# Filter maxima after the plain tiles, earlier transforms, a pipelined inverse, merged butterflies and row stores on GpSimd, in a fused FFT filter and feed-forward kernel

## The chip, the cores and the metric

The kernel runs on one core of a Trainium2 chip. Its engines are TensorE (PE, with its weight loads as PEld), VectorE (DVE), ScalarE (ACT), GpSimd (POOL) and SyncE (SP); SP, ACT and POOL also issue DMAs, each in its own order. The metric is device time in microseconds (us): the median of repeated executions on the same chip. One execution more is profiled; all rows of the profile come from that one.

## The reference

```python
def _A_ref(x, w_r, w_i):
    X = jnp.fft.rfft2(x, axes=(-2, -1))
    X = X * (w_r + 1j * w_i)
    return jnp.fft.irfft2(X, s=(S, D), axes=(-2, -1))

def _B_ref(x, w1, w2):
    h = _silu(jnp.einsum("bsd,df->bsf", x, w1))
    return jnp.einsum("bsf,fd->bsd", h, w2)

xn = _layernorm(x)                 # x: 1 x 2048 x 1024
s = _A_ref(xn, A_w_r, A_w_i)       # filters: 2048 x 513
g = _silu(_B_ref(xn, B_w1, B_w2))  # w1: 1024 x 3584, w2: 3584 x 1024
return x + s * g
```

All is float32. The kernel works on float16 pairs: each operand is split into a high and a low half, and three of the four products are added up in float32.

## The kernel before

**Feed-forward, first layer.** The 2048 tokens are four chunks c of 512, the 3584 hidden columns 28 tiles f of 128. The first 16 tiles are *plain tiles* (`mm1`, L597): for each (c, f) one psum tile pa of 24 matmuls. The other 12 are done by Strassen's scheme (`product`, L635): unit (q, g), with q from 8 to 13 and g the half of the tokens, has seven products M1 to M7 of 12 matmuls each into the psum tiles pa, pe and pc, 84 in all. M2, M3 and M1 use the normalized tokens; M4 to M7 need sums and differences of them, `T[g]`, which `t_gen` makes on DVE (L1414 to L1426) and ACT (L1427) in four rounds for each g. M1's result is copied by ACT from pa to pc (L647), and M6 goes on in pa only after that. Results pass through SiLU (ACT), DVE sums (L687 to L690) and a split (L267 on ACT, L270 on DVE), and are stored to the hd arrays by POOL.

**Second layer.** `mm2` (L737 to L739) takes pb of (m, j), seven output forms m by eight j, each in two halves k of 21 matmuls. `acc` puts the results together with the parts pd that earlier forms left (`load_parts`, L730), and `finish_out` (L811, L812) multiplies by the spatial rows s, adds x and stores the output rows (L814). For the last form m = 6 these stores and the loads of pd, of s (fs) and of x (fx) all stand on SP.

**Spatial part.** The forward transform is `fd_gen` (psum fa, by chunk) and `f_gen` (psum fx, 16 steps u of 36 matmuls, with the filter tiles xn<-in_A_w loaded by L1177 and multiplied on DVE, GpSimd and ACT). Step u is part j = u % 4 of line block q = u // 4. The last of the 513 columns, for the last block, is loaded by itself into xsv (L1179). The inverse is `i_gen(c)`, run for chunks c in the order 1, 3, 0, 2: four iu pieces (24 matmuls, two psum buffers, read by DVE L1475 and L1476), then four id pieces (24), each followed by a butterfly (L1517 to L1533, 14 DVE instructions) and the rows' stores. Its input's edge column is put in by a GpSimd copy from zp (L1456).

**Scales.** The float16 split needs the largest magnitude of each weight and filter. `wmax_gen` loads the filters as 36 pieces of 128x456, mostly two at a time, and reduces them on DVE (L1112). `w2max_gen` loads W2 in 28 tiles of 256 KB, two at a time, makes magnitudes on DVE and ACT and stores sums (L481 to L484). `w2_scales` needs the maxima of W2 before the second layer's weights can be split (`w2_gen`, tiles w2t; its loads are L535 on SP and L540 on POOL).

**What sets the order.** The program is written out by one planner in the order of PE's work. After each psum tile, `work` takes one step of the weight queue `wq`, one of `xq` (maxima) and of `sq`, and then up to three steps of `bg`, the background queue with ln, T, forward and inverse generators in this order; each step yields the DVE time that it is thought to cost, and `bg` goes on only while DVE's modelled clock is at most LEAD = 2.5 us ahead of PE's. Every engine and every DMA queue executes its own instructions strictly in the order written. So a generator that is moved in the plan moves all its instructions on all queues. `t_gen` of g = 1 may start its fourth round only when 8 plain tiles are left (`plain[0]`).

## Time and profile before

| | |
|---|---|
| median of 3 timed runs | 1318.17 us (1311.06 to 1318.68) |
| profiled execution, its own time | 1323.54 us |
| its span | 1321.8 us |
| mean granted clock of TensorE | 0.973 |
| PE busy | 1250.7 us (95%) |
| DVE busy | 996.8 us (75%) |
| ACT busy | 566.7 us (43%) |
| POOL busy | 262.7 us (20%) |
| HBM traffic | 239 GB/s over the span |

The plain tiles end at 380.3 us of the span, the Strassen products at 626.6, and the last matmul at 1304.8. Rows of a timeline read: start us, length us, engine, line, operation, output<-input (partitions x elements, type), count, and in brackets the idle time of the engine before it and what ended this. Rows of waits read: engine, tile and line, what was waited for, us in total, times, longest. A matmul's busy time has a modelled end, so the pitch of rows is a better duration than the busy time.

### The profile page before, as it was taken

The page shows a single profiled execution, that of the slowest core. Times are in us where ns is not written, and L with a number is a line of the kernel's source. Part 1 is how long each engine was busy: PE and PEld are TensorE (multiplying, and loading weights), DVE is VectorE, ACT ScalarE, POOL GpSimd, SP SyncE. Part 2 cuts the span into 40 slices and gives each one's busy share as a digit, 9 for nine tenths or more (in the row PEclk, how much of TensorE's full clock was granted, in tenths as well). Part 3 has the DMA queues.
Part 4 walks back from the last instruction along what each step waited for, and adds up shares of the span by engine and source line. Part 5 has one row for each costly group of instructions (what it writes and reads, how often), then busy time and mean ns, then how long its engine had stood idle before and what let it go on. Part 6 is the DMA issues. An engine that isn't in the chain of part 4 may idle for free.

```text
span 1321.8 us, 18630 instructions
## 1 busy us (share of the span) xinstructions
PE 1250.7 (95%) x6827; PEld 646.1 (49%) x6827; DVE 996.8 (75%) x1708; ACT 566.7 (43%) x844; POOL 262.7 (20%) x406
## 2 busy tenths in 40 slices
PE   8998999999996899999999999999899999999994
PEld 5534445444442344444545455555454455666563
DVE  6677799886997677787487859997798268687685
ACT  4854354353644788976323223332333132322221
POOL 1211253342531223332200000101126001010000
PEclk9998999999997999999999999999899989899997
DMA  7568499678546588866846688989999978685847
GB/s 239 127 171 213 125 293 310 204 177 246 134 101 148 182 256 263 274 200 213 308 143 206 203 275 207 318 233 291 224 320 293 373 251 305 231 305 213 310 139 254
DMA packets 181611, 306.68 MB, mean 232 GB/s; under 512 B 32528, under 2 KB 86288, under 8 KB 180368
## 3 DMA queue, kind: packets, MB, share of 16 engines
q1 hardware_dynamic: 137360, 169.62, 41.5%
q0 software_dynamic: 28368, 87.05, 23.6%
q10 hardware_dynamic: 15792, 48.83, 10.6%
q8 instruction: 53, 0.87, 0.3%
q14 instruction: 38, 0.31, 0.1%
HBM read 204.25 MB, written 111.67 MB: 239 GB/s over the span
## 4 chain that ended last, share of the span: by engine, by line
PE 43%; DMA 15%; DVE 7%; ACT 4%; issue 3%; POOL 1%; SPq 0%; ACTq 0%; DVEq 0%; POOLq 0%
PE pb L737 8%; PE pb L738 8%; PE pb L739 8%; PE pa L635 7%; DMA r<-in_B_w_dram 5%; PE pe L635 3%; PE iu L1466 3%; DMA pl<-pd 3%; PE fx L1193 1%; DMA xn<-vd 1%; PE id L1495 1%; PE pc L635 1%; DMA sd<-xn 1%; DMA out_dram<-pl 1%; DVE r L1419 1%
## 5 line engine op out<-in xcount | busy, mean ns | idle before, releaser
L597 PE MATMUL pa<-xn,w 128*128 128x512 f16 x1536 | 337.7, 382 | 8.8 <-DMA xn<-xs 3.7
L737 PE MATMUL pb<-r,w 128*128 128x512 f16 (+1 forms) x798 | 299.8, 376 | 0.0
L738 PE MATMUL pb<-r,w 128*128 128x512 f16 (+1 forms) x798 | 299.7, 376 | 0.0
L739 PE MATMUL pb<-r,w 128*128 128x512 f16 (+1 forms) x798 | 299.5, 375 | 0.0
L597 PEld LDWEIGHTS <-w 128*128 128x128 f16 x1536 | 150.8, 99 | 192.5 <-issue 11.8
L635 PEld LDWEIGHTS <-w 128*128 128x128 f16 x1008 | 99.7, 99 | 146.6 <-issue 25.7
L739 PEld LDWEIGHTS <-w 128*128 128x128 f16 x798 | 78.1, 98 | 91.3 <-issue 0.3
L635 PE MATMUL pa<-r,w 128*128 128x512 f16 x432 | 104.0, 390 | 18.6 <-ACT r L1427 7.7
L737 PEld LDWEIGHTS <-w 128*128 128x128 f16 x798 | 78.3, 98 | 87.6 <-issue 0.2
L738 PEld LDWEIGHTS <-w 128*128 128x128 f16 x798 | 78.2, 98 | 87.4
L267 ACT ACTIVATE r<-r,sc 128x512 f16<-128x512 f32 x88 | 61.1, 716 | 100.0 <-DMA r<-in_B_w_dram 70.7
L270 DVE SCALAR_TENSOR_TENSOR r<-r,sc 128x512 f16<-128x512 f32 x88 | 64.6, 745 | 29.1 <-ACT r L267 29.1
L681 POOL DMA_DIRECT2D hd_one<-hoone x52 | 49.4, 949 | 139.6 <-DVE hoone L270 80.3
L681 POOL DMA_DIRECT2D hd_sum<-hosum x52 | 42.0, 912 | 169.9 <-DVE hosum L270 104.4
L270 DVE SCALAR_TENSOR_TENSOR hoone<-h,hs,hoone 128x2048 f16<-128x2048 f32 x28 | 65.7, 2346 | 12.7 <-ACT hoone L267 12.5
L607 ACT ACTIVATE h<-pa,ep 128x512 f32<-128x512 f32 x64 | 43.3, 679 | 67.5 <-PE pa L597 65.3
L687 DVE TENSOR_TENSOR hr<-h 128x1024 f32<-128x1024 f32 x28 | 34.2, 1222 | 44.0 <-ACT h L607 25.9
L267 ACT ACTIVATE hoone<-h,hs 128x2048 f16<-128x2048 f32 x28 | 55.9, 1995 | 17.2 <-DMA hd_one<-hoone 15.5
L1466 PE MATMUL iu<-xn 128*128 128x256 f16 x384 | 50.6, 298 | 9.2 <-DVE xn L1476 6.2
L267 ACT ACTIVATE hosum<-hr,hs 128x1536 f16<-128x1536 f32 x28 | 43.9, 1569 | 23.7 <-DVE hr L688 13.4
L540 POOL DMA_DIRECT2D r<-in_B_w_dram x28 | 24.1, 880 | 143.3 <-DMA r<-in_B_w_dram 142.0
L1193 PE MATMUL fx<-xn 128*128 128x256 f16 x192 | 45.4, 281 | 7.2 <-DVE r L1305 5.3
(293 smaller groups left out, 2079.1 us busy)
## 6 DMA issues: line engine op xcount, KB each, us to landing
r<-in_B_w_dram SPq DMA_DIRECT2D x74, 256.0 KB, 6.8
w<-hd_dif ACTq DMA_DIRECT2D x32, 448.0 KB, 5.7
w<-hd_sum ACTq DMA_DIRECT2D x32, 448.0 KB, 6.5
w<-hd_one ACTq DMA_DIRECT2D x32, 448.0 KB, 7.2
hd_sum<-hosum POOLq DMA_DIRECT2D x52, 256.0 KB, 5.2
hd_one<-hoone POOLq DMA_DIRECT2D x52, 256.0 KB, 5.0
hd_dif<-hoone POOLq DMA_DIRECT2D x52, 256.0 KB, 4.8
xn<-in_B_w_dram SPq DMA_DIRECT2D x38, 256.0 KB, 4.1
```

Source lines behind the costliest of these rows:

```text
L267: nc.scalar.activation(hi, raw, AF.Copy, scale=scale)
L270: nc.vector.scalar_tensor_tensor(lo, raw, scale, hi, op0=OP.mult, op1=OP.subtract)
L597: nc.tensor.matmul(ps, w[:, wh, d], xt[:, xh, d], start=(n == 0), stop=(n == 23))
L607: nc.scalar.activation(hq[:, 2 * (c % 2) + f % 2], ps, AF.Silu, scale=ep[:, q:q + 1])
L635: nc.tensor.matmul(ps, lhs(d, wh), rhs(d, xh), start=(name in ("M1", "M5") and d + n == 0), stop=(d + n == 5), skip_group_check=True)
L681: defer(1, lambda k=k, m=m: stores[0].dma_start(hd[m, g][:, :, q].rearrange("f p h s -> f p (h s)"), o[:, k].rearrange("f p h s -> f p (h ...
L687: tt(sums[:, 0:2], hq[:, 0::2], hq[:, 1::2], op=OP.subtract)
L737: nc.tensor.matmul(ps, hh[:, 0], w[:, 0], start=first, stop=False)
L738: nc.tensor.matmul(ps, hh[:, 0], w[:, 1], start=False, stop=False)
L739: nc.tensor.matmul(ps, hh[:, 1], w[:, 0], start=False, stop=last)
L1193: nc.tensor.matmul(o, k[:, c, kh, 1], v[:, c, vh], start=(n == 0), stop=False)
L1466: nc.tensor.matmul(ps[:, q], lhs, rhs, start=(n == 0 and r == 0), stop=(n == 2 and r == 1))
```

## The change

Eight edits, all in one version.

1. `wmax_gen` is put on a queue of its own, `yq`, and is added when T is done (it was added at the seventh plain tile). It takes single pieces of 456 elements in two fixed buffers. `w2max_gen`, which came behind it in `xq`, so starts in the plain stage, and its Strassen part has two pairs of buffers for three, with one more step between.
2. T, which stands behind the forward transforms of the first chunks in `bg`, comes earlier, since these are partly issued ahead: `fa_mat` and `fa_evac` of the first pieces of chunks 1 and 3 are written into the end of the chunk before, and since the reductions of the filter maxima no longer take DVE's modelled time.
3. `f_gen`'s parts of the last block are taken in the order 3, 0, 1, 2 (`part_of`), and the last part is loaded with 129 columns, so that the two separate loads of one column (L1179) are dropped.
4. The inverse becomes one generator over all chunks: the first pieces of the next chunk are issued with the last ones of the one before, and the zp copy with piece 3. While it runs (`fine`), `mm2` is written in groups of 12 and 9 matmuls with one background step between.
5. The butterfly is written in 8 DVE instructions.
6. Output rows of full width are stored by POOL; half rows stay on SP and ACT.
7. `load_parts` for m = 6 is called one j ahead, and stores that are held are written out before it.
8. The loads of a chunk's zt come one step sooner.

```diff
@@ w2max_gen
-            state[1] += 2
+            state[1] += 1
+            load()
+            if aux[1] == 2:
+                yield 0
+            state[1] += 1
@@ load_parts, mm2
     def load_parts(m, j):
+        while m == 6 and held.get("pt"):
+            d = held["pt"][0]
+            slow.remove(d)
+            d[1]()
...
-    def mm2(m, j, ps, k, cols=slice(0, 512)):
-        for q in range(7):
+    def mm2(m, j, ps, k, cols=slice(0, 512), qs=range(7)):
+        for q in qs:
@@ finish_out
-        queue = nc.gpsimd if tag == "bs" else nc.scalar if cols.start and h else nc.sync
+        queue = nc.scalar if cols.start and h else nc.sync if cols.stop < 512 or cols.start else nc.gpsimd
@@ fd_gen
         for i in range(5):
-            if i < 4 and (c or i >= EARLY):
+            pre = EARLY if c in (0, 1, 3) else 0
+            if pre <= i < 4:
                 fa_mat(c, i)
-            if 1 <= i and (c or i > EARLY):
+            if pre < i:
                 fa_evac(c, i - 1)
...
+            if c in (0, 2) and j >= 2:
+                fa_mat(c + 1, j - 2)
+            if c in (0, 2) and j == 3:
+                fa_evac(c + 1, 0)
@@ wmax_gen
-            t_ = pool.tile([128, 456 * wide], F32, name=f"wm{k}", tag=tag, bufs=bufs)
-            nc.sync.dma_start(t_, src[:, 456 * (k % 18):456 * (k % 18 + wide)])
...
+        spots = Map({"y": [(R2[0], 72 * KB + 256), (R2[0], 74 * KB + 256)]})
...
+        for k in range(36):
+            if len(tl) == 2:
+                reduce()
+            src = (w_r, w_i)[k // 18].rearrange("(p r) k -> p (r k)", p=128)
+            tl.append((k, spots.tile([128, 456], F32, name=f"wm{k}", tag="y")))
+            nc.sync.dma_start(tl[-1][1], src[:, 456 * (k % 18):456 * (k % 18 + 1)])
+            yield 0.6
+            if k % 3 == 2:
                 yield 0
@@ f_gen, load_w
+    def part_of(u):
+        return u // 4, (u % 4 if u < 12 else (u - 1) % 4)
...
-        n = 129 if j == 3 and u < 15 else 128
+        n = 129 if j == 3 else 128
...
-            if u == 11:
-                nc.sync.dma_start(xsv[:, 2, 3, :, i:i + 1], wv[i][3][:, :, 512:513])
@@ load_i
-            defer(1 + n, lambda q=q: nc.sync.dma_start(zt[:, q:q + 2].rearrange("m q h r l i -> m q h (r l i)"), zd[:, q:q + 2, :, c]))
+            defer(n, lambda q=q: nc.sync.dma_start(zt[:, q:q + 2].rearrange("m q h r l i -> m q h (r l i)"), zd[:, q:q + 2, :, c]))
@@ butterfly
-            tt(s_[:, 0], pc, u, op=OP.add)
-            tt(s_[:, 4], pc, u, op=OP.subtract)
-            tt(s_[:, 2], pm_, v, op=OP.subtract)
-            tt(s_[:, 6], pm_, v, op=OP.add)
...
+            tt(s_[:, 0:8:6], pp, uv, op=OP.add)
+            tt(s_[:, 4:1:-2], pp, uv, op=OP.subtract)
@@ i_gen
+    def i_gen():
+        fine[0] = True
+        chunks = [i_chunk(c) for c in IORDER] + [None]
+        for n, (first, last) in enumerate(chunks[:-1]):
+            for i in range(2 if n else -1, 6):
+                first(i)
+                yield PAUSE
+            yield PAUSE
+            for p in range(6):
+                last(p)
+                if p >= 3 and chunks[n + 1]:
+                    chunks[n + 1][0](p - 4)
+                yield PAUSE
@@ planner
-            if n == 6:
-                add(xq, wmax_gen())
...
-            if not w2j and (w1j.done and not xq or q == NP - 1):
+            if not w2j and (w1j.done and not xq and not yq or q == NP - 1):
...
             if t_job.done and hold_x[0]:
-                aux[:] = [Map({"x": [(X1, 0), (X1, 8 * KB), (R2[0], 72 * KB + 256)]}), 3]
+                aux[:] = [Map({"x": [(X1, 0), (X1, 8 * KB)]}), 2]
                 hold_x[0] = False
+                add(yq, wmax_gen())
...
-            mm2(m, j, banks[m, j], k)
+            mm2(m, j, banks[m, j], k, qs=range(4))
+            if fine[0] and clock["dve"] <= clock["pe"] + LEAD:
+                slot(bg)
+            mm2(m, j, banks[m, j], k, qs=range(4, 7))
             if k == 0:
                 settle()
-                load_parts(m, j)
+                if m < 6:
+                    load_parts(m, j)
...
+            if m == 6 or (m, j) == (5, 7):
+                load_parts(6, (j + 1) % 8)
```

In the changed kernel the lines lie some places further down: `product` and `t_gen` by 4 to 8 (T's L1414 is L1419, L1419 is L1424), the inverse's copy L1456 is L1542, the stores L814 are L822, the loads L730 are L738 and L751 are L759, and the reduction L1112 is L1126.

Three places show how instructions move. The first is DVE at the end of T (TENSOR_TENSOR of L1414 to L1426, r and xn being its buffers). Before, these rows stand among the first Strassen units: h_8_0 is the hidden tile of unit (8, 0).

```order
L1414 TENSOR_TENSOR xn<-xn 128x1024
L1415 TENSOR_TENSOR xn<-xn 128x1024
L1419 TENSOR_TENSOR r_2848<-r_2848 128x4x512
L1423 TENSOR_TENSOR xn<-xn 128x512
L1424 TENSOR_TENSOR xn<-xn 128x512
L1425 TENSOR_TENSOR xn<-xn 128x512
L1426 TENSOR_TENSOR xn<-xn 128x512
L1419 TENSOR_TENSOR r_2848<-xn,r_2848 128x4x512
L659 TENSOR_TENSOR h_8_0_3383<-h_8_0_3383,pe_0_3363 128x512
```

The same end of T on DVE in the changed kernel, where h_7_0 and h_7_1 are of plain tiles and mw<-r_2498 is the first reduction of the filter maxima:

```order
L1431 TENSOR_TENSOR xn<-xn 128x512
L270 SCALAR_TENSOR_TENSOR hosum_7_0_3281<-hr_0_3249,hs,hosum_7_0_3281 128x12x128
L1424 TENSOR_TENSOR r_2498<-xn,r_2498 128x4x512
L270 SCALAR_TENSOR_TENSOR hoone_7_0_3317<-h_7_0_3141,hs,hoone_7_0_3317 128x16x128
L270 SCALAR_TENSOR_TENSOR w_67<-w_67,rs_222 128x1024
L270 SCALAR_TENSOR_TENSOR w_67<-r_2498,rs_222,w_67 128x1024
L691 TENSOR_TENSOR hr_1_3382<-h_7_1_3283 128x1024
L692 TENSOR_TENSOR hr_1_3382<-h_7_1_3283 128x512
L694 TENSOR_TENSOR h_7_1_3283<-h_7_1_3283 128x2x512
L270 SCALAR_TENSOR_TENSOR hosum_7_1_3395<-hr_1_3382,hs,hosum_7_1_3395 128x12x128
L270 SCALAR_TENSOR_TENSOR hoone_7_1_3409<-h_7_1_3283,hs,hoone_7_1_3409 128x16x128
L1126 TENSOR_REDUCE mw<-r_2498 128x1
```

T's last row has moved from behind the first Strassen evacuations to ahead of the last plain tiles' own rows, and the reductions now follow.

The second place is POOL in the inverse: sd are the stores of spatial rows, out_dram<-fs and <-xn the stores of output rows, zp the edge column. Before, from the second zp copy's surroundings:

```order
L814 DMA out_dram<-fs 128x512
L1544 DMA sd_1_125<-xn 128x512
L1544 DMA sd_0_124<-xn 128x512
L814 DMA out_dram<-xn 128x512
L1544 DMA sd_2_126<-xn 128x512
L1544 DMA sd_3_127<-xn 128x512
L814 DMA out_dram<-fs 128x512
L814 DMA out_dram<-xn 128x512
L1456 COPY xn<-zp 128x16
```

After, from the last w2 load of this queue on (kept are output rows of the form before the last):

```order
L544 DMA r_2498<-in_B_w_dram 128x512
L1222 DMA zd<-xn 128x4096
L1387 TENSOR_SCALAR xn<-xn 128x32
L1542 COPY xn<-zp 128x16
L822 DMA out_dram<-fs 128x512
L1537 DMA sd_1_125<-xn 128x512
L1537 DMA sd_0_124<-xn 128x512
L822 DMA out_dram<-xn 128x512
L1542 COPY xn<-zp 128x16
L1537 DMA sd_2_126<-xn 128x512
L1537 DMA sd_3_127<-xn 128x512
L822 DMA out_dram<-fs 128x512
```

The second zp copy has moved ahead of the last two row stores of its predecessor, and no w2 load stands behind a store.

The third place is the end of SP's queue: pl<-pd are `load_parts`, fs and fx the rows of s and x, out_dram the stores. Before:

```order
L814 DMA out_dram<-pl_4_2_10695 128x512
L814 DMA out_dram<-pl_4_0_10697 128x512
L730 DMA pl_7_2_11026<-pd_7_119 128x512
L730 DMA pl_7_0_11028<-pd_7_103 128x512
L751 DMA fs_3_1_11073<-sd_3_131 128x512
L751 DMA fx_3_1_11075<-in_A_x_dram 128x512
L751 DMA fs_3_0_11077<-sd_3_131 128x512
L751 DMA fx_3_0_11079<-in_A_x_dram 128x512
L814 DMA out_dram<-pl_5_2_10756 128x512
L814 DMA out_dram<-pl_5_0_10758 128x512
```

After:

```order
L738 DMA pl_7_2_10948<-pd_7_119 128x512
L738 DMA pl_7_0_10950<-pd_7_103 128x512
L759 DMA fs_2_1_10952<-sd_2_130 128x512
L759 DMA fx_2_1_10954<-in_A_x_dram 128x512
L759 DMA fs_2_0_10956<-sd_2_130 128x512
L759 DMA fx_2_0_10958<-in_A_x_dram 128x512
L759 DMA fs_3_1_11005<-sd_3_131 128x512
L759 DMA fx_3_1_11007<-in_A_x_dram 128x512
L759 DMA fs_3_0_11009<-sd_3_131 128x512
L759 DMA fx_3_0_11011<-in_A_x_dram 128x512
L822 DMA out_dram<-pl_7_2_10948 128x256
```

The loads of the last step have moved one step of rows ahead, and the full-width stores between them are gone from this queue.

107 lines of the change are left out of this document (41 added, 66 removed).

## The prediction

> **What bounds the kernel now.** I read the stages first (busy time by stretch), then TensorE's waits, then the rows around each wait. The stretches are the plain first-layer tiles, the start and the rest of the Strassen products, the second layer, and what follows the last matmul. The columns are length, busy time of PE, PEld, DVE, ACT and POOL (instructions), granted clock, DMA share, GB/s; the last row is a clean stretch of 16 products, 2.59 us each.
>
> ```profile
> 19.00:380.30 361.30, 351.15 (x1765) 165.97 (x1766) 292.10 (x433) 180.18 (x203) 114.98 (x161) 0.99 0.69 192
> 380.30:448.90 68.60, 48.68 (x192) 19.71 (x191) 53.76 (x55) 37.65 (x54) 18.21 (x24) 0.85 0.58 144
> 448.90:626.60 177.70, 176.85 (x819) 79.94 (x818) 131.30 (x160) 141.62 (x247) 49.25 (x70) 1.00 0.76 241
> 626.60:1304.80 678.20, 659.43 (x3949) 368.71 (x3947) 499.47 (x1024) 194.33 (x327) 75.79 (x134) 0.98 0.81 258
> 1304.80:1321.80 17.00, 0.04 (x1) 0.00 (x0) 9.33 (x19) 1.92 (x4) 0.00 (x0) 0.61 0.68 228
> 456.91:498.35 41.44, 41.44 (x193) 18.78 (x192) 32.36 (x39) 36.14 (x67) 13.13 (x19) 1.00 0.78 242
> ```
>
> PE is the bound nearly everywhere, so only what makes PE wait, or run slowly, costs time. TensorE's waits, longest sums first (total us, times, longest):
>
> ```profile
> PE pa L635 <- ACT r L1427: 7.7, 2, 3.9
> PE pa L635 <- ACT pc L647: 7.2, 4, 3.9
> PE iu L1466 <- DVE xn L1476: 6.2, 2, 3.1
> PE fx L1193 <- DVE r L1305: 5.3, 1, 5.3
> PE pa L597 <- DMA xn<-xs: 3.7, 2, 3.2
> PE pa L635 <- DVE r L1419: 3.7, 2, 1.9
> ```
>
> The four places that the change touches are here: the Strassen start (L635), one forward transform (fx), the inverse (iu), and the tail. A gap costs more than itself, since the granted clock is half afterwards (the two stretches that follow gaps, then an undisturbed one, each 24 matmuls for iu):
>
> ```profile
> 1067.08:1072.17 5.09, 5.09 (x24) 3.62 (x25) 3.97 (x9) 2.76 (x4) 0.00 (x0) 0.50 0.93 358
> 1077.08:1079.70 2.62, 2.62 (x26) 2.34 (x25) 2.35 (x6) 0.24 (x1) 0.00 (x0) 1.00 0.00 0
> 948.23:953.31 5.08, 5.08 (x37) 4.29 (x37) 2.79 (x8) 2.24 (x5) 0.00 (x0) 0.50 0.89 187
> ```
>
> So a gap of 3.0 us or more brings another 2.5 us (5.09 - 2.62, or half of 5.08). The Trainium skill (TensorE: Matmul & The Clock Gate, part 1 on the clock gate) has the clock at half for one busy window of about 3.4 us, a loss of 1.7 us for each gap. The trace agrees on the half (0.50) and not on the length; by the page the three gaps of the inverse below would be worth 14.3 us, by the trace 16.7.
>
> **The change part by part.** All sums are against the profiled execution: 1323.5 us, of which 1321.8 are span. It lies 5.4 us above the median of the timed runs (1318.17), so 5.4 is taken off at the end.
>
> *Strassen start (T transforms earlier).* 84 products of 2.59 us are 217.6; the two stretches are 246.3; 28.7 are lost. 177.70 us of the second stretch hold 68.6 products, so the loss lies wholly in the first 68.6 us. There PE waits for T, whose eight rounds on DVE and ACT run until 420 us:
>
> ```profile
> L1414 DVE TENSOR_TENSOR r<-xn x7: 1217/1218/1219, 321.9 to 401.5; 128x1024 f32<-128x1024 f16 x7
> L1419 DVE TENSOR_TENSOR r<-xn,r x1: 2292/2292/2292, 418.2 to 418.2; 128x2048 f16<-128x2048 f32 x1
> L1427 ACT ACTIVATE r<-r x7: 1894/1911/1912, 327.2 to 408.9; 128x2048 f16<-128x2048 f32 x7
> ```
>
> In the changed order T begins ahead of pa1_10 instead of pa2_12 and its last instruction stands among the last plain tiles, so both T waits (7.7 + 3.7) and their slow clock go. What is late next: the ACT copies of pc (7.2 in 4 waits). The first comes from M6 following M1 at once and stays, with 4.08 - 2.6 = 1.5 us of slow clock; so do two short waits for w1:
>
> ```profile
> 385.55 4.08 PE L635 MATMUL pa<-r,w 128*128 128x512 f16 x12 [2.50 <-ACT pc L647]
> 434.77 0.60 PE L635 MATMUL pa<-xn,w 128*128 128x512 f16 x2 [1.42 <-ACT w L267]
> 436.09 2.33 PE L635 MATMUL pa<-xn,w 128*128 128x512 f16 x10 [0.72 <-DVE w L270]
> ```
>
> 2.5 + 1.5 + 2.1 = 6.1 us remain, and I take 22 saved. Ends: 15, if two pc waits stay (6.4 + 2 x 2.5 + 2.1 = 13.5), and 26, if only the first does. The DVE time of T comes into the plain stage, where DVE has 292.1 of 361.3 us; the part after 380, some 3.5 of 8 rounds of 2 x 1.22 + 2.29 + 4 x 0.69 = 7.5 us each, is 26 us, and the maxima that leave make up 20 of it. The forward transforms that move ahead add no PE work.
>
> *Filter maxima behind the plain tiles.* Each tile's reduction and the landing of its load, from the trace:
>
> ```profile
> L1112 DVE TENSOR_REDUCE mw<-wm x19: 616/1093/1098, 86.0 to 261.8; 128x1 f32<-128x912 f32 x17, 128x1 f32<-128x456 f32 x2
> wm<-in_A_w_i_dram SPq DMA_DIRECT2D x9, 456.0 KB, 5.2
> wm<-in_A_w_r_dram SPq DMA_DIRECT2D x8, 456.0 KB, 7.3
> ```
>
> 17 x 1.09 + 2 x 0.62 = 19.8 us of DVE leave the plain stage; 36 x 0.62 = 22 come into the Strassen stage, where DVE is idle for 177.7 - 131.3 = 46 us. The cover holds if the reductions do not wait. With two buffers a load is followed by its own reduction 2, 3 and 3 products later, in turn: 5.2, 7.8, 7.8 us. A reduction that waits holds DVE, behind it the additions of M3 and M7 and ACT's SiLU, and behind those ACT's pc copy, for which PE waits. At the landings above only every third tile of w_r waits, 6 x 2.1 = 13 us, inside the 24 us that DVE has left. SP is held too: a load waits for the reduction that frees its buffer, with the loads of W2 (w2max, now two buffers for three) behind it. Price: 2 us taken, up to 50 (all 36 landing at 9 us: 12 x 3.8 + 24 x 1.2 = 74, less 24). A gain is possible only where the loads that leave the plain stage slowed others: PE's wait there for the transposed tokens (DMA xn<-xs, 3.7, with 2.5 of slow clock 6.2) may shrink, so that the other end is -6.2; nothing shows that it does. The Trainium skill (DMA: Bandwidth & Descriptors, anatomy of one DMA) fits a DMA of the GpSimd path with 2.0 us plus its bytes at 436 GB/s, which for 228 KB would be an estimated 2.5 us, and no reduction would ever wait; the price would be 0, the sum 1268, and rivals B and D below would fall. This trace has 5.2 and 7.3 for such loads from SP, so they stand.
>
> *Forward transform.* fx12's wait of 5.3 and half clock (2.5) make 7.8 us. Its DVE inputs wait for an ACT queue that waits for w2 tiles, and the DMA rings there move little while nearly always busy, just when two loads of 4-byte pieces are under way:
>
> ```profile
> 902.00:924.00 22.00, 22.00 (x128) 11.30 (x126) 14.13 (x25) 6.32 (x11) 3.46 (x5) 1.00 1.05 316
> 924.00:942.00 18.00, 18.00 (x109) 9.47 (x108) 12.12 (x20) 4.07 (x7) 3.38 (x4) 1.00 0.96 166
> L1179 SPq DMA_DIRECT2D xsv<-in_A_w_i_dram x1: 1283/1283/1283, 926.2 to 926.2; - x1
> DMA to landing us min/median/max: 15.0/17.6/20.1
> ```
>
> The change reads those columns with a row of 129 elements, so the tiny loads (15 and 20 us to landing) go. I take 7 saved; ends 0 (the rings are full at 902 too) and 8. That the transforms start half a step earlier adds nothing to PE.
>
> *Inverse.* Three waits: two for DVE L1476 (6.2 in all; two buffers, third or later iu) and one for the copy of zp, which stands on POOL behind a store that waits for DVE. Ahead of the second L1476 wait DVE itself waits for a pd load:
>
> ```profile
> 1125.07 6.19 PE L1466 MATMUL iu<-xn 128*128 128x256 f16 x29 [3.00 <-POOL xn L1456]
> ```
>
> ```profile
> 1124.21 0.54 POOL L814 DMA_DIRECT2D out_dram<-xn  x1 [7.81 <-DVE xn L812]
> 1124.75 0.27 POOL L1456 COPY xn<-zp 128x16 f16<-128x16 f16 x1
> 1241.07 0.69 DVE L797 TENSOR_TENSOR pl<-pl,pb 128x512 f32<-128x512 f32 x1 [3.67 <-DMA pl<-pd]
> ```
>
> 9.2 us of gaps and 3 x 2.5 of slow clock are 16.7. In the new order 12 or 9 matmuls (2.59 or 1.94 us) stand between iu pieces: from the end of iu1_0 to iu1_2 there are 1.94 + 2.62 + 2.59 = 7.2 us where DVE needed 2.6 + 3.1 = 5.7. The zp copy of the next chunk comes a chunk early, but still behind row stores on POOL, 12 matmuls before iu3_0; the pd loads come a step early. I take 12 saved, one gap being left or new somewhere; ends 16.7 and -5.5 (four gaps for three). POOL's queue now holds all full-width stores, each waiting for DVE; queued behind them are only zp copies and stores of the spatial rows, and the last w2 loads of that queue are issued ahead of the first store.
>
> *Merged butterflies.* From the rows
>
> ```profile
> L1517 DVE TENSOR_TENSOR xn<-id,xn x16: 415/424/425, 1092.3 to 1288.6; 128x256 f32<-128x256 f32 x16
> L1526 DVE TENSOR_TENSOR xn<-xn x16: 281/283/287, 1093.9 to 1290.3; 128x128 f32<-128x128 f32 x16
> ```
>
> 4 x 0.42 + 10 x 0.28 = 4.5 us become 8 instructions: two of twice 0.42 at the most, two of 0.28, four of 0.42, 3.9 us. That is 0.6 us sixteen times, on an engine that is not the bound: 0.
>
> *Tail.* SP issues the last pd loads late, behind stores that wait for DVE; the second half of the last step is handled from 1316.07 to 1318.86 and the span ends 2.9 us later:
>
> ```profile
> 1301.71 0.91 SPq L814 DMA_DIRECT2D out_dram<-pl  x2
> 1307.06 0.96 SPq L730 DMA_DIRECT2D pl<-pd  x2
> 1316.07 0.41 DVE L797 TENSOR_TENSOR pl<-pl,pb 128x256 f32<-128x256 f32 x1
> 1318.44 0.42 DVE L812 TENSOR_TENSOR pl<-pl,fx 128x256 f32<-128x256 f32 x1
> ```
>
> With the loads a step early and the stores on POOL, these 5.7 us can follow PE's end nearly at once: between 6 and 9 us after it, 7.5 taken, of 17.0. Saved 9.5, ends 8 and 11.
>
> Sum: 22 - 2 + 7 + 12 + 9.5 = 48.5; 1323.5 - 48.5 = 1275.0, less 5.4: **1269.6, say 1270**.
>
> **Rivals.** B: the reductions wait and the Strassen gain goes. At landings of 8.3 us, 12 x 3.1 + 24 x 0.5 = 49 us of waits, 25 beyond DVE's idle time: 1270 + 23 = 1293. For it: DMA is 0.76 busy there and 6 MB more come in (36 tiles of 228 KB, less eight of 256 KB for w2 that move ahead), so landings grow; against: most of the 36 have 7.8 us. C: the inverse and fx12 keep their waits, elsewhere: 19 us back, 1289. For it: POOL's queue and a DVE that bunches; against: DVE's mean load there, 169 of 231 us:
>
> ```profile
> 1058.64:1289.20 230.56, 221.38 (x1370) 137.33 (x1370) 169.16 (x408) 60.18 (x90) 13.01 (x26) 0.96 0.72 250
> ```
>
> B and C together give 1312. The change not doing what it says is T still arriving late since DVE, more loaded in the plain stage, falls behind its order: 22 back and some gap at the plain tiles, with C's losses 1311; it counts in the same case. D, slower: the same reductions, at landings like those of the filter tiles in the second layer:
>
> ```profile
> xn<-in_A_w_i_dram SPq DMA_DIRECT2D x13, 256.0 KB, 10.9
> ```
>
> Then 12 x 5.7 + 24 x 3.1 = 143 us of waits, 119 beyond DVE's idle time, some 1387. It decides from 85 us of waits on (24 idle, 48 of gains, 13 to leave the uncertainty), a mean landing of 9.3 us. Against it: those 10.9 belong to a stretch with DMA at 1.0.
>
> **How the numbers follow.** The forecast 0.60, B 0.16, C 0.13, B and C together or T late 0.07, D 0.04. One per cent, about what a measurement tells from no change, is 13 us: faster is under 1305. The forecast, C and nearly all of B lie there (0.86); same takes the 0.07 and the edge of B (0.10); D is slower (0.04). Low end: all upper ends, 26 + 6.2 + 8 + 16.7 + 11 = 67.9 saved, 1250. High end 1299, past B and C; 0.13 is left out above.
>
> **What would show it.** In the profile after: PE without waits for T lines in the first 70 us of Strassen, and that stage at about 226 us; the reductions of the maxima with idle time under 20 us before them; no gap at fx12; at most one gap over 2.4 us at iu; 7 to 8 us from the last matmul to the end. Wrong it would be by waits of PE for ACT's pc copy spread over all Strassen units (B, D), or by new waits for zp or L1476 (C).

## The result, and the profile after

The changed kernel takes 1295.43 us (median of 4; 1292.91 to 1299.27), the kernel before 1315.03 (median of 4): the ratio is 0.9854, 95% interval 0.9810 to 0.9899, so it is 1.5% faster, by 19.6 us. The forecast was 1270, with a range of 1250 to 1299: the time lies in the range, near its upper end, and the saving is two fifths of the 48.5 us that were added up.

The profiled executions differ by more: 1323.54 us before, 1292.91 after. The one of before lies 8.5 us above its median, the one after 2.5 below. By stretches of the two profiles (us; a stage ends where the next one's first matmul starts):

| stretch | before | after | saved | forecast |
|---|---|---|---|---|
| to the first Strassen product | 380.3 | 374.2 | 6.1 | 0 |
| Strassen products (217.6 needed) | 246.3 | 243.0 | 3.3 | 22 - 2 |
| second layer to the last matmul | 678.2 | 664.2 | 14.0 | 7 + 12 |
| after the last matmul | 17.0 | 9.7 | 7.3 | 9.5 |
| sum | 1321.8 | 1291.1 | 30.7 | 48.5 |

The same stretches in the view of busy time of the changed kernel (columns as in the prediction):

```profile
19.00:374.18 355.18, 348.37 (x1765) 165.32 (x1764) 303.20 (x435) 199.90 (x240) 114.82 (x165) 1.00 0.71 191
374.18:617.19 243.01, 225.58 (x1010) 100.08 (x1009) 175.38 (x228) 159.38 (x262) 65.61 (x92) 0.96 0.74 223
617.19:1281.40 664.21, 652.90 (x3949) 365.42 (x3947) 497.80 (x936) 196.02 (x329) 93.83 (x155) 0.99 0.84 266
1281.40:1291.10 9.70, 0.00 (x0) 0.00 (x0) 4.21 (x10) 0.91 (x2) 0.54 (x1) 0.61 0.50 190
```

TensorE's waits in the changed kernel, longest sums first:

```profile
PE pa L639 <- ACT h L655: 8.3, 2, 4.2
PE pa L639 <- ACT pc L651: 6.0, 4, 4.4
PE eps L1341 <- POOL xn L1334: 3.5, 1, 3.5
PE pa L639 <- ACT h L653: 3.1, 2, 2.8
PE fx L1200 <- DVE xn L1295: 2.9, 1, 2.9
PE pa L601 <- DVE w L270: 2.4, 1, 2.4
...
PE pa L601 <- DMA xn<-xs: 1.3, 1, 1.3
```

All waits for T's lines (7.7 + 3.7 us before) and all waits at iu (6.2 + 3.0) are gone, and xs has 1.3 us for 3.7. The second layer in two parts, up to the first iu and from there to the last id, first of the kernel before, then of the changed one:

```profile
626.60:1058.60 432.00, 422.40 (x2467) 220.41 (x2465) 320.79 (x594) 131.37 (x233) 62.13 (x107) 0.99 0.86 261
1058.60:1286.30 227.70, 218.53 (x1356) 135.94 (x1356) 166.86 (x398) 59.58 (x89) 12.60 (x25) 0.96 0.72 250
```

```profile
617.19:1045.70 428.51, 417.24 (x2437) 217.59 (x2436) 320.51 (x593) 131.42 (x232) 68.56 (x107) 0.99 0.86 263
1045.70:1242.80 197.10, 197.10 (x1294) 126.43 (x1293) 154.74 (x306) 57.76 (x86) 19.57 (x38) 1.00 0.78 273
```

The inverse's part now runs without a gap and at full clock. The parts hold other numbers of matmuls, so the lost time is an estimate: the length less each part's matmuls at the pitch of undisturbed rows (0.216 us for 512 columns, 0.109 for 256, 0.056 for 128). It was 17.1 us in the inverse's part and is nothing; ahead of it, it was 11.8 and is 14.8.

In the place of T's waits, PE waits 17.4 us in the Strassen stage for ACT copies (L651, L653, L655). What those copies stand behind on ACT and DVE is in the waits of these engines, of the changed kernel:

```profile
ACT both L289 <- DMA xn<-in_B_w_dram: 13.3, 8, 4.6
ACT both L289 <- DMA r<-in_B_w_dram: 12.8, 4, 7.3
DVE mw L1126 <- DMA r<-in_A_w_r_dram: 10.4, 6, 2.7
DVE mw L1126 <- DMA r<-in_A_w_i_dram: 6.8, 3, 3.5
```

and of the kernel before, where ACT's L289 waited for W1 only this much, for W2 not at all, and DVE for no filter piece:

```profile
ACT both L289 <- DMA r<-in_B_w_dram: 0.5, 2, 0.4
```

L289 takes sums of magnitudes: xn are W2's tiles, r those of W1; mw are the reductions of the filter maxima. One gap, in the changed kernel's timelines of ACT, SP and PE:

```profile
455.13 0.63 ACT L289 ACTIVATE both<-r 128x512 f16<-128x512 f32 x1 [7.26 <-DMA r<-in_B_w_dram]
...
456.51 0.58 ACT L655 ACTIVATE h<-pa 128x512 f32<-128x512 f32 x1
```

```profile
447.69 2.55 SPq L405 DMA_DIRECT2D r<-in_B_w_dram  x2
450.35 2.92 SPq L1133 DMA_DIRECT2D r<-in_A_w_r_dram  x1
```

```profile
457.14 4.44 PE L639 MATMUL pa<-r,w 128*128 128x512 f16 x12 [4.19 <-ACT h L655]
```

Two W1 loads are issued from 447.7 on, ACT reaches their sums before they have landed and stands for 7.26 us, and the copy that frees pa, ready to go, comes when the sums are done. PE stands for 4.19 us and then runs slowly: 12 matmuls take 4.3 us to the next row instead of 2.6.

### The profile page after: what moved, and what is told of

The parts are those of the page before. It is cut to its first block, busy times and chain, and to the rows that moved or that the text cites. A ratio compares the mean times of both kernels' runs of the same rounds, so it can differ in the third digit from the quotient of the medians.

```text
span 1291.1 us, 18582 instructions
## 1 busy us (share of the span) xinstructions
PE 1242.7 (96%) x6827; PEld 643.3 (50%) x6827; DVE 991.6 (77%) x1628; ACT 567.6 (44%) x844; POOL 279.3 (22%) x428
## 3 DMA queue, kind: packets, MB, share of 16 engines
q0 software_dynamic: 30128, 92.82, 25.4%
q10 hardware_dynamic: 15792, 48.83, 10.7%
## 4 chain that ended last, share of the span: by engine, by line
PE 50%; DMA 10%; DVE 6%; issue 4%; ACT 3%; POOL 1%; SPq 0%; ACTq 0%; DVEq 0%; POOLq 0%
PE pb L745 11%; PE pb L746 11%; PE pb L747 11%; PE pa L639 5%; DMA r<-in_B_w_dram 3%; PE id L1496 3%; PE iu L1467 3%; PE pe L639 2%; DMA xn<-in_B_w_dram 2%; DMA ws<-xn 1%; DMA r<-in_A_w_r_dram 1%; PE pc L639 1%; PE fx L1200 1%; DMA hd_one<-hoone 1%; ACT both L289 1%
## 5 line engine op out<-in xcount | busy, mean ns | idle before, releaser
L639 PEld LDWEIGHTS <-w 128*128 128x128 f16 x1008 | 100.1, 99 | 142.9 <-issue 27.7
L639 PE MATMUL pa<-r,w 128*128 128x512 f16 x432 | 105.7, 397 | 17.4 <-ACT h L655 8.3
L270 DVE SCALAR_TENSOR_TENSOR hosum<-hr,hs,hosum 128x1536 f16<-128x1536 f32 x28 | 50.7, 1812 | 4.8 <-ACT hosum L267 4.8
L1496 PE MATMUL id<-xn 128*128 128x256 f16 x384 | 44.5, 273 | 0.0
```

What stands on the lines that cost most here:

```text
L270: nc.vector.scalar_tensor_tensor(lo, raw, scale, hi, op0=OP.mult, op1=OP.subtract)
L639: nc.tensor.matmul(ps, lhs(d, wh), rhs(d, xh), start=(name in ("M1", "M5") and d + n == 0), stop=(d + n == 5), skip_group_check=True)
L1496: nc.tensor.matmul(o, us[g][:, uh, 2 * p + r], C["ci"][:, ch, g, r], start=(n == 0 and r == 0), stop=(n == 2 and r == 1))
```

## The experiments

Each kernel is the changed one with the edit shown; `...` stands for lines of the edit that are left out. Ratios are to the kernel before (its medians in these comparisons are 1312.6 to 1315.9), to be set against the changed kernel's 0.9854. Second layers are given from the first pb to the start of the last matmul, 663.9 us in the changed kernel. Strassen stages that were left alone came out at 243.0 to 245.7 us in the profiles of six kernels (the changed one, 4, 8, 12, 15, 16), second layers that were left alone at 664 to 669, so differences under 3 and under 6 us are not read there. The busy-time rows below are each kernel's Strassen stage; the second number is its length.

### What holds the Strassen stage

**1. No filter loads.**

```diff
-            nc.sync.dma_start(tl[-1][1], src[:, 456 * (k % 18):456 * (k % 18 + 1)])
+            if k < 2:
+                nc.gpsimd.memset(tl[-1][1], 0.3)
```

> The changed kernel without the 36 loads of filter pieces: the 36 reductions stay and read two buffers filled with a constant, so the filter maximum is a constant here. In the changed kernel the Strassen stage takes 243.0 us (374.18 to 617.19) of which 217.6 are the products. Theory SP: a load of a piece waits on SP for the reduction that frees its buffer, the loads of W1 and W2 stand behind it, ACT waits for those in order (L289: 26 us) and its copies for PE come late; then the stage falls to 222 to 226 us, ACT's waits at L289 to under 6, and the time by 17 to 21 us. Theory DVE: the reductions' own waits (17.2 us, 9 times) hold the additions; the same fall here, since these waits go too. Rival two buffers: W2's loads are late because their tiles have two pairs of buffers fewer, whatever the filter does; the stage stays at 238 to 245.

```profile
374.90:607.90 233.00, 223.80 (x1010) 99.82 (x1009) 174.69 (x228) 159.25 (x262) 66.57 (x94) 0.98 0.65 197
```

1284.85 us (ratio 0.9768, 0.9728 to 0.9809). The maxima's loads cost 10 us of the stage, half of what both theories gave; ACT still waited 14.6 us at L289, for W1 and W2.

**2. Filter loads on GpSimd.**

```diff
-            nc.sync.dma_start(tl[-1][1], src[:, 456 * (k % 18):456 * (k % 18 + 1)])
+            nc.gpsimd.dma_start(tl[-1][1], src[:, 456 * (k % 18):456 * (k % 18 + 1)])
```

> The changed kernel with the 36 loads of filter pieces issued by GpSimd instead of SyncE; all waits between loads and reductions stay. Theory SP: SP no longer stands still, ACT's waits at L289 fall from 26 to under 10 us, the Strassen stage from 243 to 224 to 230, the time by 12 to 18 us. Theory DVE: the reductions still wait 15 to 25 us, the stage stays at 240 to 246 and the time within 4 us. Rival two buffers: also no change. A new cost can be that GpSimd's stores of hidden tiles wait behind such a load: then POOL shows waits for L1126 and DVE or ACT waits for hd stores.

```profile
375.80:625.10 249.30, 225.42 (x1010) 99.91 (x1009) 175.24 (x228) 159.26 (x262) 85.12 (x128) 0.97 0.73 218
```

1302.01 us (0.9903, 0.9870 to 0.9936). ACT's L289 waits fell to 16.6, much as with no filter loads, yet the stage grew by 6: the reductions on DVE now waited 32.0 us for 17.2. Against theory SP; for theory DVE, though waits, stage and time all went past the numbers it gave. GpSimd itself stood 63.7 us for reductions, but no wait of DVE or ACT for stores of hidden tiles came of it. Why the pieces come later on this queue was not taken apart.

**3. The first edit undone** (maxima in the plain stage, three pairs for w2max).

```diff
...
+            if n == 6:
+                add(xq, wmax_gen())
...
-                aux[:] = [Map({"x": [(X1, 0), (X1, 8 * KB)]}), 2]
+                aux[:] = [Map({"x": [(X1, 0), (X1, 8 * KB), (R2[0], 72 * KB + 256)]}), 3]
                 hold_x[0] = False
-                add(yq, wmax_gen())
```

> The changed kernel with the first edit undone alone: the filter maxima are taken in the plain stage again and w2max has its three pairs of buffers in the Strassen stage; all other edits stay. By the written order T then ends at the second Strassen product again instead of ahead of the last plain tiles. Theory that early T needs the maxima out of the plain stage: PE waits for T lines return (5 to 15 us with slow clock), ACT's L289 waits go (26 to under 4), so that the Strassen stage is 228 to 240 and the plain stage 3 to 6 us longer (its wait for xs returns); time within 8 us of the changed kernel, either side. Theory that the early transforms alone bring T forward: no T waits and no L289 waits, stage 222 to 226, time 12 to 18 us below the changed kernel.

TensorE's waits in this kernel:

```profile
PE pa L635 <- ACT r L1437: 8.5, 1, 8.5
PE pa L635 <- ACT pc L647: 8.2, 4, 5.7
PE pa L597 <- ACT hoone L267: 4.9, 1, 4.9
```

1299.44 us (0.9885, 0.9853 to 0.9918). Late T is back (L1437 is T's ACT line), the plain stage is 5 us longer (products from 379.3), the Strassen stage 242.4, above the 240 expected. So it is the maxima leaving the plain stage that brings T forward; in the Strassen stage late T costs as much as the late loads of the changed kernel. But ACT's L289 still waits 8.7 us here, 8.1 of them for W1, and part of the wait for T is one of these:

```profile
405.29 0.69 DVE L1436 TENSOR_TENSOR xn<-xn 128x512 f32<-128x512 f32 x1
...
407.55 0.63 ACT L289 ACTIVATE both<-r 128x512 f16<-128x512 f32 x1 [6.39 <-DMA r<-in_B_w_dram]
410.66 1.89 ACT L1437 ACTIVATE r<-xn 128x2048 f16<-128x2048 f32 x1
```

DVE has T's input for L1437 ready at 406.0, and ACT takes it at 410.66, after the sums over the W1 tiles that came late. So about 4.7 of the 8.5 us that PE stands for T come from W1's loads.

**5. No maxima, three pairs for w2max.**

```diff
...
-        spots = Map({"y": [(R2[0], 72 * KB + 256), (R2[0], 74 * KB + 256)]})
...
-        for k in range(36):
...
+        nc.vector.memset(mt, 0.3)
...
-                aux[:] = [Map({"x": [(X1, 0), (X1, 8 * KB)]}), 2]
+                aux[:] = [Map({"x": [(X1, 0), (X1, 8 * KB), (R2[0], 72 * KB + 256)]}), 3]
```

> The changed kernel without any work on the filter maxima (no loads, no reductions; the maximum is a constant) and with the three pairs of buffers that w2max had before. The first experiment, with no filter loads but two pairs, still lost 15.4 us of its 233.0 in the Strassen stage, with ACT waiting 14.6 us at L289 for W1 and W2. Theory two buffers: those waits come from SP standing at a W2 load whose pair of buffers is not free; with three the stage is 221 to 226 us and ACT's L289 waits are under 5. Rival: the rest belongs to the products themselves (M6 right behind M1, ACT 80% busy) and the stage stays at 230 to 234.

```profile
373.80:605.50 231.70, 220.34 (x1009) 98.90 (x1008) 156.06 (x193) 158.86 (x262) 65.61 (x92) 0.99 0.65 198
```

1282.41 us (0.9761, 0.9742 to 0.9779). ACT waits for W2 no longer, but the stage is as in experiment 1: ACT still waits 10.5 us for W1. The number is the rival's; its reason, that the rest belongs to the products, does not hold by 13.

**6. Loads kept, reductions left out.**

```diff
+        nc.vector.memset(mt, 0.3)
...
-            k, t_ = tl.pop(0)
-            nc.vector.tensor_reduce(mt[:, k:k + 1], t_, axis=AX.X, op=OP.max, apply_absolute_value=True)
+            tl.pop(0)
```

> The changed kernel with its 36 loads of filter pieces but without the 36 reductions (the maximum is a constant): SP still waits, now for the landing of the load before into the same buffer, and DVE waits for none. Theory DVE, for which the second experiment speaks (loads off SP, reductions waiting 32 us instead of 17, the stage 249.3): what the filter maxima cost is the time that the reductions hold DVE; the stage falls to that of the first experiment, 231 to 235. Theory SP: it stays at 239 to 245 with L289 waits of 20 us or more.

```profile
375.40:608.70 233.30, 220.68 (x1010) 98.99 (x1008) 156.25 (x193) 158.65 (x262) 65.63 (x92) 0.99 0.76 232
```

1285.35 us (0.9786, 0.9765 to 0.9806). The loads are all there, SP still waits for landings, L289 still waits 23.4 us, and the stage is that of experiment 1. The maxima cost by way of DVE. In 1 the reductions' work is there and their loads and waits are gone (DVE busy 174.7 us), here the work is gone too (156.3): the stage is the same, so in this state it is the waits that cost, not the work.

**9. W1 sums two steps later.**

```diff
+            if k > 1:
+                yield 0
+                yield 0
             for i in range(2):
                 magnitude(r[i].rearrange("p a b -> p (a b)"), ma[:, 2 * i:2 * i + 2])
```

> The changed kernel in which, from the third pair of W1 tiles on, two more steps lie between the loads of a pair (L405) and the ACT sums over it (L289). Theory W1: besides the filter maxima, ACT waits in order for these loads (r<-in_B_w: 7.3 and 4.7 us in the changed kernel, 0.5 in all before), since early T lets the W1 work run ahead on the queue; its copies h and pc then come late (gaps of 4.19 and 4.14 at 457 and 500). With the steps between, ACT's L289 waits for r fall from 12.8 to under 4, the gaps at 457 and 500 to under 2.5 each, the Strassen stage from 243 to 234 to 239, the time by 3 to 8 us. Rival: the wait moves to the filter reductions or to W2's loads; within 3 us.

The waits of ACT and DVE in it:

```profile
ACT both L289 <- DMA xn<-in_B_w_dram: 18.0, 9, 5.4
```

```profile
DVE mw L1129 <- DMA r<-in_A_w_i_dram: 16.4, 6, 9.2
DVE mw L1129 <- DMA r<-in_A_w_r_dram: 11.3, 5, 3.3
```

1298.03 us (0.9871, 0.9835 to 0.9906), stage 243.9: nothing gained. The W1 waits are gone, and those for W2 and of the reductions (27.7 for 17.2) have grown in their place.

**10. Maxima at five steps for three pieces** (four in the changed kernel).

```diff
-            if k % 3 == 2:
+            if k % 3:
                 yield 0
```

> The changed kernel in which the filter pieces are taken at five steps for three (four for three before), so that the reduction stands 3, 4 and 3 products behind its load instead of 2, 3 and 3; buffers, loads and reductions are the same. Theory DVE: the cost of the maxima (10 us of the stage by the first and sixth experiments) is the waiting of the reductions (17.2 us); it falls under 6 us, and the stage to 234 to 238, the time by 5 to 9 us. Rival: the cost is the 22 us of DVE work itself in a stage that is already tight, or the loads' DMA traffic; then the stage stays within 3 us of 243.

```profile
374.60:612.70 238.10, 224.72 (x1010) 99.92 (x1009) 175.11 (x228) 158.89 (x262) 66.54 (x92) 0.97 0.75 228
```

1292.53 us (0.9822, 0.9786 to 0.9858). The same work with the reductions waiting 9.6 us instead of 17.2 (under 6 was expected) makes the stage 4.9 us shorter; in the second layer this execution loses it again. The work is unchanged, so here too it is the waits that cost.

**11. Experiments 9 and 10 and the edge column of experiment 4 together.**

> Both of these together with the edge column's later beginning. If the two costs in the Strassen stage add up and nothing takes their place, the stage is 226 to 232 us, the second layer 2 us shorter, the time 1274 to 1283 us. If one hides the other, the stage is 234 or more and the time 1284 or more.

1288.00 us (0.9793, 0.9759 to 0.9827), but the stage is 243.5: the second of the two expectations came. The reductions still wait 11.3 us here. One gap of 7.8 us stands where W2's tiles, taken in two pairs of buffers, come late:

```profile
420.46 0.69 DVE L484 TENSOR_TENSOR xn<-xn 128x512 f32<-128x512 f32 x1 [6.21 <-DMA xn<-in_B_w_dram]
```

```profile
424.23 2.29 PE L642 MATMUL pa<-r,w 128*128 128x512 f16 x5 [7.82 <-ACT pc L654]
```

**13. All three away** (the edits of 5 and 9).

> The changed kernel without any work on the filter maxima (the maximum is a constant), with three pairs of buffers for w2max, and with two more steps between the W1 loads and their sums. Theory: three kinds of late loads hold ACT by turns, and each hides the others, so that only all three together free the stage: 221 to 225 us (217.6 and the first pair of M1 and M6), ACT's L289 waits under 3 us, time 1272 to 1277. Rival: ACT's own load (80% busy) is what is left; the stage stays at 229 to 232 like the fifth experiment's 231.7.

```profile
374.30:597.70 223.40, 218.46 (x1009) 98.49 (x1008) 155.85 (x193) 159.13 (x262) 65.26 (x92) 1.00 0.69 205
```

1277.47 us (0.9724, 0.9683 to 0.9765). ACT has the same 159 us of work as in the changed kernel, waits 2.8 us at L289, and the stage is 5.8 us above the products' own 217.6. So late W1, late W2 and the filter maxima are 19.6 us of the loss of 25.4, and each hid the others: late W1 alone, which gained nothing in 9, is worth 8.3 us here against 5. With the waits of the reductions this kernel also leaves out their 22 us of DVE work. That the work costs nothing is shown only while the other waits stand (1 and 6).

**14. A full kernel with the three mended:** three pairs for w2max, the maxima behind it with six buffers and two pieces a product, the edits of 9 and 4.

```diff
-                aux[:] = [Map({"x": [(X1, 0), (X1, 8 * KB)]}), 2]
+                aux[:] = [Map({"x": [(X1, 0), (X1, 8 * KB), (R2[0], 72 * KB + 256)]}), 3]
...
-        spots = Map({"y": [(R2[0], 72 * KB + 256), (R2[0], 74 * KB + 256)]})
+        spots = Map({"y": [(X1, 0), (X1, 2 * KB), (X1, 8 * KB), (X1, 10 * KB), (R2[0], 72 * KB + 256), (R2[0], 74 * KB + 256)]})
...
-            if len(tl) == 2:
+            if len(tl) == 6:
...
+            if not xq and not wm_job:
+                wm_job.append(add(yq, wmax_gen()))
```

> A full kernel: the changed one with three pairs of buffers for w2max, the filter maxima behind w2max with six buffers and two pieces per product, the W1 sums two steps later, and the edge column one step later. By the theory of three late loads the Strassen stage is 222 to 228 us, the second layer 662 us, the time 1270 to 1279. Rival: the maxima, now in the last third of the stage, meet the first work on the second layer's weights, and a gap of 5 us or more appears after 560 us; 1280 or more.

```profile
375.80:605.60 229.80, 220.86 (x1009) 98.91 (x1008) 174.90 (x228) 159.26 (x262) 67.24 (x92) 0.99 0.77 236
```

1278.58 us (0.9729, 0.9680 to 0.9777): 2.7% below the kernel before, and with an interval wholly below that of the changed kernel. The stage is 13 us shorter, 1.8 us above the upper end of what was expected and 6.4 above that of 13, which has no maxima; a gap of 8.1 us at an fx (PE waits for DVE kept L787) has come in the second layer. An earlier form, **7**, with one piece a product and without the edits of 9 and 4, had let the maxima run into the second layer's scales:

> The changed kernel with three pairs of buffers for w2max, and the filter maxima begun when w2max is through, with all six freed buffers of 2 KB instead of two, so that a load stands five pieces ahead of its reduction. If the two costs found (reductions that wait, w2max with two pairs) are all: reductions wait under 4 us in all, the Strassen stage is 221 to 228 us instead of 243, the time 15 to 20 us below the changed kernel, 1275 to 1281. Rival: the maxima, now later and one per product, hold up the first weights of the second layer, which PE then waits for at the stage's end; under 8 us gained.

1296.46 us (0.9864, 0.9837 to 0.9890), stage 242.0. The rival came in place and size, though what PE stood for was not a weight: DVE was at the last reductions and scales, ACT behind it, and PE waited 7.0 us at 587 for ACT's h (L649); the W1 waits were still there (10.6 us).

### The other edits

**4. Edge column one step later.**

```diff
-            if u >= 13:
+            if u >= 14:
                 next(edge, None)
...
```

> The changed kernel with the edge column's work begun one step u later (14 instead of 13). Theory edge: with parts 3, 0, 1, 2 the last input of the edge column comes at u = 13 and the matmuls eps stand right behind its GpSimd copies, so PE waits 3.5 and then 1.4 us and runs slowly after it (9.4 us from the end of fx14 to pb4_7 where the matmuls need about 1.3); one step later the copies are done and the second layer is 7 to 9 us shorter, the time 6 to 9 us. Rival: the wait is set by DVE, which is late for all of this stage, and only moves: under 3 us of change.

1289.23 us (0.9807, 0.9769 to 0.9844). The wait at eps is 2.4 us, for DVE, and one of 3.9 has grown at an fx (for vd); the second layer is 2 us shorter, less than can be read. The time fell by 6, the profiled span by 3. The wait moved at least in part; the two theories stay undecided.

**15. Parts in the old order.**

```diff
-        return u // 4, (u % 4 if u < 12 else (u - 1) % 4)
+        return u // 4, u % 4
...
+                nc.sync.dma_start(xsv[:, 2, 3, :, i:i + 1], wv[i][3][:, :, 512:513])
```

> The changed kernel with the third edit undone alone: the last block's parts in the order 0, 1, 2, 3 and the two loads of one column back. Theory: the forecast saw the waits before fx12 (7.8 us with slow clock) go and nothing come; in the changed kernel eps waits instead (3.5 and 1.4 us, and slow clock). Undone, the wait at eps goes and one of 4 to 6 us at an fx comes; the second layer is within 3 us of 663.9, so that the edit is worth nothing by itself. Rival: the tiny loads cost as the forecast had it, 5 us or more longer.

```profile
PE fx L1202 <- DVE r L270: 5.1, 1, 5.1
```

1294.40 us (0.9852, 0.9803 to 0.9902); second layer 664.9 us for 663.9. The wait at eps is gone, fx waits 5.1 and 3.0 us instead, iu 3.2. No worth of the edit can be seen here.

**16. Transforms late.**

```diff
-            pre = EARLY if c in (0, 1, 3) else 0
+            pre = EARLY if c == 0 else 0
...
-            if c in (0, 2) and j >= 2:
-                fa_mat(c + 1, j - 2)
...
```

> The changed kernel with the second edit undone alone: the first pieces of chunks 1 and 3 are issued with their own chunk again; the maxima stay behind the plain tiles. By the written order T still ends among the last plain tiles. Theory: what brings T forward is the 20 us of reductions that left the plain stage; the plain stage and the Strassen stage stay within 2 us each, the time within 4 us. Rival: the early pieces are needed; T waits of PE of 5 us or more come back, the time 6 us or more above.

```profile
PE fx L1194 <- DMA xn<-vd: 8.4, 2, 5.7
PE eps L1335 <- POOL xn L1328: 7.6, 1, 7.6
```

1303.91 us (0.9919, 0.9894 to 0.9944). Products begin at 375.9 and take 244.1 us: T needs no early transforms, as expected. But the second layer is 13.7 us longer, at fx and eps, and neither theory had it: in the changed kernel the early pieces are needed there. That is no gain against the kernel before, which does not issue these pieces ahead and lost 11.8 us in front of the inverse, where the changed kernel loses 14.8. This kernel and that of 12 do not compute the whole output rightly; they have the same number of matmuls (6827), but their waits may not be those of a right kernel in the same order.

**12. No step between the groups of matmuls.**

```diff
-            if fine[0] and clock["dve"] <= clock["pe"] + LEAD:
-                slot(bg)
```

> The changed kernel without the background step between the two groups of matmuls of a half of pb, so that the inverse's pieces follow each other at whole halves again (21 matmuls); the pipelining over chunks stays. Theory: the room between iu pieces is what took away the waits for L1476 and for zp; 2 or 3 gaps of about 3 us with half clock behind them come back at iu, and the second layer is 8 to 16 us longer. Rival: the pipelining over chunks alone does it, no gaps come back, within 3 us.

```profile
PE iu L1467 <- DVE xn L1518: 7.2, 2, 4.2
PE iu L1467 <- DVE xn L1477: 3.0, 2, 2.1
```

```profile
1057.30:1240.00 182.70, 182.70 (x1085) 106.08 (x1084) 115.50 (x216) 49.50 (x74) 9.29 (x18) 1.00 0.80 271
1240.00:1307.70 67.70, 52.20 (x336) 36.12 (x334) 49.55 (x99) 11.68 (x17) 5.68 (x11) 0.82 0.49 162
```

1336.17 us (1.015, 1.011 to 1.019). The second layer is 33 us longer, not 8 to 16, and the gaps do not come back where they were expected. For the first three chunks, where one piece and one half of 21 matmuls take turns, PE has no gap at all, as the rival had it. The gaps come in the last chunk, from 1263 on, where the four iu pieces follow each other with nothing between them; in the kernel before, the two waits for L1476 stand at a third iu piece in direct sequence too. Each piece of the new inverse takes one step, and without the added steps the inverse is late: its last matmuls start 9 us ahead of the last one of all instead of 38, and the tail is 20.4 us. So what the trace speaks for is that the pieces must not follow each other directly, and that the added step is needed for the inverse to end in time. As this kernel's output is not right (see 16), it is not shown.

**8. Row path undone.**

```diff
-        queue = nc.scalar if cols.start and h else nc.sync if cols.stop < 512 or cols.start else nc.gpsimd
+        queue = nc.gpsimd if tag == "bs" else nc.scalar if cols.start and h else nc.sync
...
-            if m == 6 or (m, j) == (5, 7):
-                load_parts(6, (j + 1) % 8)
```

> The changed kernel with the last edits of the row path undone: full-width rows of the last forms stored by SP again and the parts for m = 6 loaded with their own j. Theory: from the last matmul to the end 16 to 18 us instead of 10.0; and with the loads late again a wait of DVE for pd (3.7 us before) comes back ahead of the inverse's reads, which the new interleaving has room for; time 6 to 9 us above the changed kernel. Rival: the inverse's wait comes back too, 11 to 14 us above. Rival: the tail is bound by the last stores and not by these loads, within 3 us.

Its last loads on SP:

```profile
1283.95 0.98 SPq L734 DMA_DIRECT2D pl<-pd  x2
```

1300.07 us (0.9892, 0.9875 to 0.9910). From the start of the last matmul to the end 11.2 us, in the changed kernel 10.0, in the kernel before 17.2. The last matmul starts at 1287.2, so the loads still come 3 us ahead of it; before they came 2.5 us behind it (1307.06 against 1304.6). So the queues are 1.2 us of the 7.2, within what the tails of the other kernels differ by (8.0 to 10.7, without 12). The rest goes with the inverse's end: its last matmuls start 18 us ahead of the last one of all before, 38 us in the changed kernel and here, and 9 us in 12, whose tail is 20.4. An edit that moves the inverse's end alone was not run.

## Why the prediction was wrong

The forecast missed by 25.8 us (1295.4 against 1269.6): 17.8 of it in the stages (48.5 against 30.7), 8 in the offset.

- **Strassen start: the step that failed is the one after T.** That T's waits would go was right, but the stage still loses 25.4 us (28.7 before), where 6.1 was to remain. The forecast named what is late next as ACT's pc copies and took them for a cost of the first pair alone. It did not look at what stands on ACT ahead of those copies, the W1 and W2 sums at L289, which wait 26.1 us for their loads, 0.5 before. This term was 22 and had nothing for it; W1 alone is worth 8.3 us (5 against 13). Why these loads are late now stays open: W1's loads land after 6.5 us in the middle for 5.2 before, but that T's waits had given them time does not fit 3, where T is late and they are waited for 8.1 us. The 5.8 us that 13 keeps are near the forecast 6.1 by luck: its first pc wait is 0.7 us for 2.5, a copy of h has 2.4, and the waits for w are gone. The upper end, 26, leaves out the 1.5 us of slow clock that the middle counts for the same wait.
- **Filter maxima: priced at 2 us, measured at 10.** The mechanism was rival B's: reductions that wait for their pieces hold DVE, then ACT, then PE. The reductions waited 17.2 us, near the 13 worked out, though from landings of pieces twice as large (456 KB for 228). The sign given for a success, under 20 us of idle time before them, was met and cost 10 us all the same. The failed step is that "the 24 us that DVE has left" would take this in: idle time elsewhere in the stage does not help an engine that must go on now. Taking loads (1) or reductions (6) away gave 10 us each; the waits halved (10) gave 4.9. SP's part, named in the same paragraph, cost nothing measurable.
- **w2max with two pairs** had no price in the sum. By experiments 1 and 5 it is 1.3 us alone, less than can be read; in 11, where the W1 waits are gone and the reductions still wait 11.3 us, PE's longest gap (7.8 us) stands where its tiles are late. The three costs replace each other, so their sum can't be read from the profile of the whole.
- **Plain stage: 0 taken, 6.1 measured**, at the other end given (6.2): PE's wait for xs fell from 3.7 to 1.3 us, and with the maxima back (3) the stage is 5 us longer again, with PE's wait at that place for ACT (4.9 us).
- **Forward transform: 7 taken, none measured** (3 lost, less than can be read). The tiny loads were near the wait of fx12 in time, but experiment 15 has them back and the stage the same: the waits at fx and eps replace each other. The early pieces, costed at nothing, keep this part from losing 13.7 us more (16). The forecast gave 19 for fx and inverse, the second layer has 14.0.
- **Inverse: 12 taken, 17 measured:** no gap is left at iu, where one was allowed for, and the mechanism is the one stated, room between iu pieces. By the trace of 12, a kernel whose output is not right, halves of 21 matmuls are room enough, and the added step is what lets the inverse end in time. One reading was off: the third iu gap of the kernel before is followed by 4.30 us for 24 matmuls, a loss of 1.7 and not 2.5.
- **Tail: 9.5 taken, 7.3 measured,** for another cause than stated: the stores on GpSimd and the early loads make 1.2 us (8); that the rest is the inverse's earlier end is argued from the traces of 8 and 12.
- **Merged butterflies and the earlier loads of zt** were not tried apart.
- **The offset.** 5.4 us were taken off since the profiled execution of before was so much above its median. The one after lies 2.5 below its own: the offset belonged to one execution.

Rivals: B's 1293 us is near the 1295.4 measured, in part by luck. The reductions did wait and the Strassen gain went, but B had 49 us of waits from landings of 8.3 us; there were 17.2, from landings of 4.7 us in the middle and 8.4 at the longest, and W1 and W2 did the rest. Of C the part on the forward transform happened, the part on the inverse did not. D did not happen.

## What to carry to other kernels

Before pricing a removed wait at its full length, list what else was due in its shadow: every load whose consumer stands on an in-order engine ahead of what the bound engine needs. Work that waits for a load is not hidden by an engine's idle time but by the distance between load and use; count that distance against the longest landing, not the middle one (here 5.2 us against landings of 4.7 in the middle and 8.4 at the longest). When several such loads share queues, take them all away once in an experiment, since each alone hides behind the others.

## What the runs showed of the hardware

After a gap the half clock cost TensorE different amounts: 2.5 us over the first 24 matmuls after two of the iu gaps of the kernel before (5.09 us for 2.62), but 1.7 us at its third (4.30) and 1.7 us at the gap at 457 in the changed kernel (12 matmuls in 4.3 us instead of 2.6). The granted clock shows the difference: it was 0.50 for 6.8 us around the first iu gap, for 3.4 us around the third, and for 3.4 us after the gap at 457, with 1.00 next to these stretches. Two rows of the kernel before, then one of the changed one:

```profile
1066.10:1072.90 6.80, 5.82 (x26) 3.93 (x27) 5.68 (x13) 2.76 (x4) 0.00 (x0) 0.50 0.84 313
1247.00:1250.40 3.40, 3.40 (x18) 2.35 (x17) 2.28 (x4) 1.54 (x2) 0.00 (x0) 0.50 0.69 208
```

```profile
457.50:460.90 3.40, 3.40 (x10) 1.18 (x8) 2.74 (x3) 3.34 (x6) 0.00 (x0) 0.50 0.50 171
```

The Trainium skill (TensorE: Matmul & The Clock Gate, part 1 on the clock gate) has a free-running window of 3.4 us, from which a loss of 1.7 us a gap is an estimate. The second and third rows agree, the first is twice as long as it gives.

The profiled execution of the kernel before took 1323.5 us, 3 us more than the longest of 13 timed executions of a later comparison (1309.4 to 1320.6); the changed kernel's profiled execution was the shortest of its four.
